# Batch 0's Q and K in thirds, w1 and w2 in quarters, and a first phase in another order

## The chip, the cores and the metric

The kernel runs on one core of a Trainium2 chip. The metric is the time of one execution in microseconds, measured on the device. A core has five engines that work through their own queues in order: TensorE (PE; its weight loads are PEld), VectorE (DVE), ScalarE (ACT), GpSimd (POOL) and SyncE (SP). They wait for each other by semaphores only. Transfers between HBM and SBUF run beside them on 16 DMA engines; an engine's queue only issues them.

## The reference

Attention over a sliding window of 64 tokens, then a feed-forward block that multiplies two projections:

```python
scores = (1 / np.sqrt(64)) * np.matmul(q, k.transpose(0, 1, 3, 2))   # q, k, v: 8 batches, 8 heads, 576 tokens, 64
rel = pos[:, None] - pos[None, :]
scores = np.where((rel >= 0) & (rel < 64), scores, -1e9)
attn = softmax(scores)
x = np.matmul(attn, v)              # laid out as 4608 tokens x 512
h = ((x @ w1) * (x @ w2)) @ w3      # w1, w2: 512 x 1024, w3: 1024 x 1024
out = h @ w_out                     # w_out: 1024 x 512, out: 4608 x 512, fp32
```

All inputs are fp32 in HBM. The kernel computes in fp16 with fp32 accumulation. Since nothing stands between `w3` and `w_out`, it folds them once into one matrix `wc = w3 @ w_out` (1024 x 512).

## The kernel before

The work has three kinds. **Attention** goes by batch; a batch has three segments of 192 query tokens (`SEGS`), and a segment two halves of four heads, numbered d = 0 to 47. For segment n, `scores(n)` multiplies K and Q into two PSUM tiles; `weigh(d)` takes Exp of one half on ACT and zeroes what lies outside the window, on POOL by two selects (`select`) or on DVE by one multiply with a band of ones and zeros (`bands`, made by `make_bands`); `values(d)` multiplies with V and, through Ln, Exp(-x) and a multiply on DVE, writes normalized columns of `xT`. V's tiles `v16s` hold ones beside V (`ones_of`), so that the row sums come out of the same matmuls. `copy_v` builds V blocks that overlap others. `keep_sums` writes the logarithms of the sums to a small tile on SP's queue, for a check at the end.

**Folding** (once): `fold_t(fc)` transposes a row block of w3 on PE (8 matmuls with the identity) and copies it out of PSUM; `fold_mm(fc, c0, c1, cp)` multiplies it with w_out into columns of `wc_sb`, and `cp` says which engine takes the result out of PSUM.

**Feed-forward** goes by group g of 512 tokens, nine in all: `ffn_ab(g, fc)` computes one block of 128 columns of both projections (64 matmuls of 512 columns for a whole group), copies one to SBUF on ACT and multiplies on DVE; `ffn_o(g, t)` multiplies 128 tokens with `wc_sb`, and `store` writes them out on SP's queue. `ffn_ab` and `fold_*` share four PSUM buffers (`ps_f`), `scores` and `values` share two (`ps_a`).

**Q and K** come in head pairs: `load_qk` loads a batch by four transfers per tensor (32 partitions each), converting to fp16 on the way, which POOL's queue does; `transposes(b, which, hh)` turns 32x32 blocks on DVE, one call per tensor and half hh (576 tokens), into `kT` and `qT`.

**Order.** Nothing is scheduled automatically (`manual_schedule`): each engine gets its instructions in the order of the Python calls. Every load that converts is issued by POOL. The loads share eight semaphores in turn, so a load waits at POOL for the landing of the load eight before it. The first phase, lines 516 to 619, is written out call by call: loads, `keep_busy(120)` (matmuls of the identity with itself, whose result nobody reads), scores of batch 0, folding, values, the first group's `ffn_ab`, and batch 1's attention between the first group's `ffn_o`. From line 622 on a loop takes over: `slots` lists what is left of the feed-forward with a due tick each, and `tick(u)` runs attention four ticks per segment between them, its loads by the table `late`.

Of the kernel before, what the change touches and what calls it, by code (L numbers as in the profile page):

```python
# [8 lines left out]
FP32 = mybir.dt.float32  # L9
# [135 lines left out]
def kernel(  # L145
# [25 lines left out]
    EARLY = 2  # L171
# [28 lines left out]
    RUN = [9] * 3 + [2] * (B - 3)  # L200

    def load_qk(b, which, *hhs):
        src = k if which == "k" else q
        r = RUN[b]
        if (which, b) not in t16s:
            t16s[which, b] = sb.tile([P, 2, TI * D], FP16, name=which + "16", bufs=2)
        t = t16s[which, b]
        if not hhs:
            for j in range(NJ):
                nc.gpsimd.dma_start(  # L210
                    out=t[32 * j:32 * j + 32].rearrange("p hh (i n) -> p (hh i) n", n=r * D),
                    in_=src[b, 2 * j:2 * j + 2].rearrange("hh (i p r) d -> p (hh i) (r d)", p=32, r=r))
        for hh in hhs:
            for i in range(2):
                nc.gpsimd.dma_start(
                    out=t[:, hh, i * r * D:(i + 1) * r * D],
                    in_=src[b, hh:H:2, i * 32 * r:(i + 1) * 32 * r].rearrange("j (p r) d -> j p (r d)", p=32, r=r))

    def transposes(b, which, hh):

        dst = kTs if which == "k" else qTs
        r = RUN[b]
        if hh == 0:
            dst[b] = sb.tile([P, 2, S, 2], FP16, name=which + "T")
        nc.vector.transpose(  # L225
            dst[b][:, hh].rearrange("q t c -> q (t c)").bitcast(I32).rearrange("q (i p r) -> q i r p", p=32, r=r),
            t16s[which, b][:, hh].bitcast(I32).rearrange("p (i r e) -> p i r e", r=r, e=32))
# [44 lines left out]
    def scores(n, now=True):  # L272
# [19 lines left out]
        weigh(2 * n)  # L292
        if now:
            weigh(2 * n + 1)

    def weigh(d):
# [9 lines left out]
        if d % 2 == 1 and d < 6 * EARLY:  # L306
# [7 lines left out]
    def values(d):  # L314
# [7 lines left out]
        o_ps = ps_a.tile([P, 2, 512], FP32, name="a_ps")  # L322
        if jp == 0:
            lns[b, si] = sb.tile([P, NJ, 192], FP32, name="ln_s", bufs=4)
        y = lns[b, si][:, j0:j0 + 2]
        r = sb.tile([P, 2, 192], FP32, name="r")
        x0 = (b * S + q_base) % RING
        xs = xT[:, j0:j0 + 2, x0:x0 + 192]
        if b < SHORT:
# [12 lines left out]
            o, total = (o_ps[:, e, 0:384].rearrange("p (j n) -> p j n", j=2) for e in range(2))  # L342
            nc.scalar.activation(y, total, AF.Ln)
            nc.scalar.activation(r, y, AF.Exp, scale=-1.0)  # L344
            nc.vector.tensor_tensor(xs, o, r, ALU.mult)  # L345
            return
        for jj in range(2):
            first = True
            for a in range(2):
                c0 = 0  # L350
                for bi, (k0, q0, n, _) in enumerate(seg):
# [6 lines left out]
                    c0 += n  # L358
        nc.scalar.activation(y[0:D], o_ps[D:P, :, 0:192], AF.Ln)  # L359
# [23 lines left out]
    def tick(u):  # L383
# [3 lines left out]
        if m == 0 and n < NS:  # L387
            scores(n, now=False)
        if m == 1 and n < NS:
            weigh(2 * n + 1)  # L390
        if m in (1, 2) and 6 < n <= NS:
            values(2 * n - 3 + m)
        for e in late.get(r, []):
            event(b, *e)
# [59 lines left out]
    def load_w12(i, half):  # L454
        cols = slice(half * 512, half * 512 + 512)
# [3 lines left out]
    def load_wo(half):  # L459
        cols = slice(half * 256, half * 256 + 256)  # L460
        nc.gpsimd.dma_start(out=wo16[:, :, cols], in_=moe_w_out[:, cols].rearrange("(e p) m -> p e m", p=P))  # L461

    def load_w3(n):
        fc = 2 * n
        dst = w3a[:, 2 * fc:2 * fc + 4, :].rearrange("p (f a) n -> p f (a n)", f=2) if n < 2 else \
            xT[:, fc - 4:fc - 2, 2 * S:2 * S + DF]
        nc.gpsimd.dma_start(out=dst, in_=moe_w3[fc * P:fc * P + 2 * P].rearrange("(f p) n -> p f n", p=P))

    def fold_t(fc):
# [6 lines left out]
        dve_cp(w3Ts[fc], tp)  # L476
# [49 lines left out]
    for i in range(2):  # L526
# [10 lines left out]
    load_w3(3)  # L537
    load_v(0, 4, 5)
    fold_mm(0, 0, 256, act_cp)
    fold_mm(1, 0, 256, act_cp)  # L540
    fold_t(2)
    fold_t(3)
    scores(2)
    for i in range(2):
        load_w12(i, 0)
    fold_mm(2, 0, 256, act_cp)
    fold_mm(3, 0, 256, act_cp)
    fold_mm(0, 256, DM, act_cp)
    fold_mm(1, 256, DM, act_cp)
    fold_t(4)  # L550
    fold_t(5)
    fold_mm(2, 256, DM, act_cp)
    fold_mm(3, 256, DM, act_cp)
    copy_v(0, 1)
    fold_mm(4, 0, DM, act_cp)
    values(0)
    values(1)
    fold_t(6)
    fold_mm(5, 0, DM, act_cp)
    values(2)  # L560
    values(3)
    copy_v(0, 4)
    fold_t(7)
    fold_mm(6, 0, DM, act_cp)
    values(4)
    values(5)
    fold_mm(7, 0, DM, act_cp)
    for i in range(2):
        load_w12(i, 1)
    load_qk(1, "k")  # L570
    load_qk(1, "q")
# [115 lines left out]
```

## Time and profile before

| what | us |
|---|---|
| median of 3 runs (268.27 to 270.63) | 268.4 |
| profiled execution | 268.59 |
| its span, first to last instruction | 266.8 |
| PE busy | 254.4 |
| DVE / ACT / POOL busy | 169.7 / 151.4 / 178.7 |

HBM is read for 38.8 MB and written for 9.44 MB. The granted clock of TensorE is 0.997 of full speed over the span.

How to read it: a row names the line of the kernel, the engine, the operation, and out<-in by the program's names with partitions x elements; x120 is the number of instructions. Times in the timeline and in the chain are microseconds from the start of the span. In square brackets stands how long the engine stood idle just before, and what ended the idle time. Matmuls are pipelined: a row's length is from the first start to the last end, and the next row can start before it ends. The line "GB/s" gives bytes as written (fp16 in SBUF) in 40 equal slices of the span, 6.67 us each. The tile names `ab` and `xT` of DMA rows in the first phase are w3 and w_out: their fp16 copies lie in buffers that are used otherwise later. L506 is `keep_busy`, L474 `fold_t`, L481 `fold_mm`, L286 `scores`, L337 the matmuls of `values`, L417 those of `ffn_ab`, L435 those of `ffn_o`, L225 the transposes on DVE, L210 the loads of Q and K.

### The profile page before, as it was taken

The page shows a single profiled execution, that of the slowest core. Times are in us where ns is not written, and L with a number is a line of the kernel's source. Part 1 is how long each engine was busy: PE and PEld are TensorE (multiplying, and loading weights), DVE is VectorE, ACT ScalarE, POOL GpSimd, SP SyncE. Part 2 cuts the span into 40 slices and gives each one's busy share as a digit, 9 for nine tenths or more (in the row PEclk, how much of TensorE's full clock was granted, in tenths as well). Part 3 has the DMA queues.
Part 4 walks back from the last instruction along what each step waited for, and adds up shares of the span by engine and source line. Part 5 has one row for each costly group of instructions (what it writes and reads, how often), then busy time and mean ns, then how long its engine had stood idle before and what let it go on. Part 6 is the DMA issues. An engine that isn't in the chain of part 4 may idle for free.

```text
span 266.8 us, 6600 instructions
## 1 busy us (share of the span) xinstructions
PE 254.4 (95%) x2608; PEld 149.7 (56%) x2608; DVE 169.7 (64%) x260; ACT 151.4 (57%) x261; POOL 178.7 (67%) x243
## 2 busy tenths in 40 slices
PE   3979999998999999999999999999999999999992
PEld 3968654445886445545556984545455445444441
DVE  6644454978775675986687567668786565564531
ACT  1037474367656577758874855777498748342300
POOL 7979826679879999999898739687766345005000
PEclk9999999999999999999999999999999999999998
DMA  5999999999999999899999765998540040012013
GB/s 81 170 207 186 189 207 201 131 181 138 149 106 62 131 206 77 61 165 162 62 106 180 102 43 64 202 105 57 99 96 4 7 150 6 0 53 108 0 57 109
DMA packets 75380, 29.45 MB, mean 110 GB/s; under 512 B 62369, under 2 KB 69793, under 8 KB 75345
## 3 DMA queue, kind: packets, MB, share of 16 engines
q0 software_dynamic: 69920, 19.41, 74.9%
q1 hardware_dynamic: 5280, 9.46, 10.0%
q8 instruction: 21, 0.34, 0.6%
q14 instruction: 15, 0.11, 0.2%
q10 hardware_dynamic: 144, 0.13, 0.1%
HBM read 38.80 MB, written 9.44 MB: 181 GB/s over the span
## 4 chain that ended last, share of the span: by engine, by line
PE 87%; DMA 4%; POOL 2%; DVE 2%; ACT 2%; issue 1%; POOLq 0%; DVEq 0%
PE f_ps L417 48%; PE f_ps L435 22%; PE a_ps L353 5%; PE a_ps L286 4%; PE f_ps L481 4%; DMA ab<-in_moe_w_dram 4%; PE a_ps L337 3%; ACT pt L303 1%; PE f_ps L474 1%; POOL q L210 1%; POOL k L210 1%; DVE xT L345 1%; DVE kT L225 1%; POOL ab L461 0%; DVE pt L308 0%
## 5 line engine op out<-in xcount | busy, mean ns | idle before, releaser
L417 PE MATMUL f_ps<-xT,w_sb 128*128 128x512 f16 (+1 forms) x704 | 131.5, 341 | 0.0
L417 PEld LDWEIGHTS <-w_sb 128*128 128x128 f16 x704 | 66.3, 98 | 50.7 <-issue 0.2
L423 DVE TENSOR_TENSOR ab<-f_ps,a_sb 128x512 f16<-128x512 f32 x72 | 49.6, 689 | 33.0 <-PE f_ps L417 31.2
L303 ACT ACTIVATE pt<-a_ps 128x1024 f16<-128x1024 f32 (+1 forms) x48 | 44.5, 953 | 45.4 <-PE a_ps L286 45.4
L258 POOL TENSOR_SCALAR_AFFINE_SELECT pt<-pt 128x1024 f16<-128x1024 f16 (+2 forms) x56 | 46.1, 824 | 30.6 <-ACT pt L303 30.5
L435 PE MATMUL f_ps<-wc_sb,ab 128*128 128x512 f16 (+1 forms) x296 | 66.4, 374 | 0.0
L422 ACT COPY a_sb<-f_ps 128x512 f32<-128x512 f32 x72 | 41.8, 581 | 36.9 <-PE f_ps L417 36.4
L260 POOL TENSOR_SCALAR_AFFINE_SELECT pt<-pt 128x1024 f16<-128x1024 f16 (+2 forms) x56 | 46.5, 831 | 3.9
L435 PEld LDWEIGHTS <-ab 128*128 128x128 f16 x296 | 27.3, 98 | 28.8
L238 POOL DMA_DIRECT2D v<-in_v_dram x40 | 34.0, 860 | 1.0 <-issue 0.4
L362 DVE TENSOR_TENSOR xT<-a_ps,r 64x384 f16<-64x384 f32 x30 | 16.5, 550 | 22.0 <-ACT r L361 22.0
L437 DVE COPY t2k<-f_ps 128x512 f32<-128x512 f32 (+1 forms) x35 | 23.7, 679 | 8.4 <-PE f_ps L435 7.9
L210 POOL DMA_DIRECT2D q<-in_q_dram x32 | 19.7, 621 | 11.8 <-DMA w_sb<-in_moe_w_dram 8.3
L210 POOL DMA_DIRECT2D k<-in_k_dram x32 | 20.1, 634 | 1.6 <-POOLq L671 1.0
L353 PEld LDWEIGHTS <-v 128*128 128x128 f16 x240 | 15.1, 98 | 6.4
L345 DVE TENSOR_TENSOR xT<-a_ps,r 128x384 f16<-128x384 f32 x18 | 10.0, 553 | 13.0 <-ACT r L344 13.0
L359 ACT ACTIVATE ln_s<-a_ps 64x384 f32<-64x384 f32 x30 | 14.6, 487 | 5.8 <-PE a_ps L353 5.0
L353 PE MATMUL a_ps<-pt,v 128*128 128x128 f16 x240 | 17.2, 215 | 0.0
L363 DVE TENSOR_TENSOR xT<-a_ps,r 64x384 f16<-64x384 f32 x30 | 16.8, 561 | 0.4
L286 PEld LDWEIGHTS <-kT 32*128 32x128 f16 x768 | 10.9, 92 | 9.6 <-issue 9.3
L361 ACT ACTIVATE r<-ln_s 128x384 f32<-128x384 f32 x30 | 15.7, 523 | 1.0
L225 DVE STREAM_TRANSPOSE qT<-q 128x576 int32<-128x576 int32 x16 | 14.7, 928 | 1.6 <-DMA q<-in_q_dram 1.6
(44 smaller groups left out, 184.9 us busy)
## 6 DMA issues: line engine op xcount, KB each, us to landing
out_dram<-t2k SPq DMA_DIRECT2D x35, 256.0 KB
k<-in_k_dram POOLq DMA_DIRECT2D x32, 144.0 KB, 6.3
q<-in_q_dram POOLq DMA_DIRECT2D x32, 144.0 KB, 5.8
v<-in_v_dram POOLq DMA_DIRECT2D x32, 128.0 KB, 5.0
w_sb<-in_moe_w_dram POOLq DMA_DIRECT2D x4, 512.0 KB, 9.7
ab<-in_moe_w_out_dram POOLq DMA_DIRECT2D x2, 512.0 KB, 9.5
ab<-in_moe_w_dram POOLq DMA_DIRECT2D x2, 512.0 KB, 9.4
xT<-in_moe_w_dram POOLq DMA_DIRECT2D x2, 512.0 KB, 10.4
```

Source lines behind the costliest of these rows:

```text
L210: nc.gpsimd.dma_start(out=t[32 * j:32 * j + 32].rearrange("p hh (i n) -> p (hh i) n", n=r * D), in_=src[b, 2 * j:2 * j + 2].rearrange("hh ...
L238: nc.gpsimd.dma_start(out=vh[lo:P, c], in_=v[b, :, s0:s0 + P - lo, :].rearrange("h s d -> s h d"))
L258: nc.gpsimd.affine_select(out=sl, in_=sl, pattern=pat, compare_op=ALU.is_ge, fill=0.0, base=off, channel_multiplier=-1)
L260: nc.gpsimd.affine_select(out=sl, in_=sl, pattern=[[-s, m] for s, m in pat], compare_op=ALU.is_ge, fill=0.0, base=63 - off, channel_multip ...
L286: nc.tensor.matmul(s_ps[j // 2][:, j % 2, o0:o0 + m], kT[part, a, k0:k0 + P, c], qT[part, a, q0:q0 + m, c], start=(c == 0), stop=(c == 1), ...
L303: nc.scalar.activation(pt[:, :, :, 0:w], s_ps, AF.Exp, bias=-SHIFT, scale=scale)
L353: nc.tensor.matmul(o_ps[:, jj, o0:o0 + n], v16[:, si * 2 + bi, j0 + jj, a * D:a * D + P], pt[:, jj, a, c0:c0 + n], start=first, stop=(bi = ...
L417: nc.tensor.matmul(d[:, f * n + c0:f * n + c1], w[:, dc, (fc + f) * P:(fc + f + 1) * P], xT[:, dc, xc:xc + c1 - c0], start=first, stop=(dc ...
L422: act_cp(a_sb[:, 0:nf * n], a_ps[:, 0:nf * n])
L423: nc.vector.tensor_tensor(ab[:, fc:fc + nf, lo:hi], b_ps[:, 0:nf * n].rearrange("p (f n) -> p f n", f=nf), a_sb[:, 0:nf * n].rearrange("p ...
L435: nc.tensor.matmul(o_ps[:, 0:c1 - c0], ab[:, fc, t * P:t * P + P], wc_sb[:, fc, c0:c1], start=(fc == 0), stop=(fc == 7))
L437: cp(o_sb[:, c0:c1], o_ps[:, 0:c1 - c0])
```

## The change

Batch 0's Q and K are cut into three thirds of 192 tokens (`RUN[0]` is 6 instead of 9). The first third of each tensor and half is loaded as fp32 without conversion, three of the four by SP's queue and one by ACT's, into a part of w1's tile (`room_of`); `cast` converts it on DVE or ACT. The other thirds come converted, by POOL (`load_third`). `transposes` can do one third. w1 and w2 are loaded in quarters of 256 columns instead of halves, w3 in five pieces instead of four. `values` is split: `norm` is a call of its own, made right behind it in the loop, so that nothing changes there. `weigh` gets its engine as an argument; batch 0 and 1 now have eight of twelve halves on DVE instead of six. `fold_t` gets the engine of its copy. One of the two memsets of ones goes to POOL. The first phase is laid out anew; the loop from tick 24 on is the same.

```diff
-    RUN = [9] * 3 + [2] * (B - 3)
+    RUN = [6] + [9] * 2 + [2] * (B - 3)
...
+    def third(b, which, hh, i):
+        r = RUN[b]
+        src = k if which == "k" else q
+        return src[b, hh:H:2, i * 32 * r:(i + 1) * 32 * r].rearrange("j (p r) d -> j p (r d)", p=32, r=r)
+
+    def room_of(which, hh, i):
+        n = RUN[0] * D
+        y = 2 * "kq".index(which) + hh
+        return (w1_sb, w2_sb)[i].rearrange("p a n -> p (a n)").bitcast(FP32)[:, y * n:(y + 1) * n]
...
+    def load_raw(which, hh, i, queue):
+        queue.dma_start(out=room_of(which, hh, i), in_=third(0, which, hh, i))
+
+    def cast(which, hh, i, cp):
+        n = RUN[0] * D
+        cp(t16_of(0, which)[:, hh, i * n:(i + 1) * n], room_of(which, hh, i))
+
+    def load_third(b, which, hh, i):
+        n = RUN[b] * D
+        nc.gpsimd.dma_start(out=t16_of(b, which)[:, hh, i * n:(i + 1) * n], in_=third(b, which, hh, i))
...
-        if d % 2 == 1 and d < 6 * EARLY:
+        if engine is nc.vector:
...
-    def load_w12(i, half):
-        cols = slice(half * 512, half * 512 + 512)
+    def load_w12(i, c0, c1):
+        cols = slice(c0, c1)
...
-    load_qk(0, "k")
+    load_w3(0, 1)
     make_identity(nc, ident16)
-    load_qk(0, "q")
-    load_wo(0)
-    load_w3(0)
+    load_w3(1, 1)
+    load_raw('k', 1, 0, nc.sync)
     make_bands()
-    load_w3(1)
-    load_wo(1)
-    load_w3(2)
-    load_v(0, 0, 2, 3)
-    for i in range(2):
-        ones_of(i, nc.vector)
-    for which in "kq":
-        for hh in range(2):
-            transposes(0, which, hh)
-    keep_busy(120)
-    scores(0)
-    keep_busy(30)
-    fold_t(0)
-    fold_t(1)
+    load_w3(2, 2)
+    load_raw('q', 1, 0, nc.sync)
+    load_wo(0, 256)
+    ones_of(1, nc.gpsimd)
+    load_third(0, 'q', 1, 1)
+    load_raw('k', 0, 0, nc.sync)
+    keep_busy(85)
+    cast('k', 1, 0, dve_cp)
+    load_wo(256, 512)
+    load_third(0, 'k', 0, 1)
+    load_raw('q', 0, 0, nc.scalar)
+    cast('q', 0, 0, dve_cp)
+    transposes(0, 'q', 0, 0)
+    load_w3(4, 2)
...
+    fold_t(0, act_cp)
+    fold_t(2, act_cp)
...
+    fold_t(1, dve_cp)
...
+    keep_busy(20)
+    fold_t(3, act_cp)
+    keep_busy(20)
+    fold_mm(2, 0, 256, act_cp)
+    load_third(0, 'q', 0, 2)
     scores(0)
+    weigh(0, nc.vector)
+    fold_mm(0, 0, 256, dve_cp)
+    transposes(0, 'k', 0, 1)
+    fold_mm(1, 0, 256, dve_cp)
...
+    load_w12(1, 512, 768)
+    values(3)
+    load_qk(1, 'k')
+    norm(3)
+    load_qk(1, 'q')
+    fold_mm(7, 0, DM, act_cp)
+    load_w12(0, 768, 1024)
+    fold_mm(6, 0, DM, act_cp)
+    load_w12(1, 768, 1024)
     scores(2)
+    load_qk(2, 'k')
+    weigh(4, nc.vector)
+    weigh(5, nc.vector)
+    ffn_ab(0, 0, 2, 0, 256)
+    values(4)
+    load_v(1, 0)
+    norm(4)
+    ffn_ab(0, 2, 2, 0, 256)
+    keep_sums(0)
+    values(5)
+    norm(5)
+    transposes(1, 'k', 0)
+    ffn_ab(0, 4, 2, 0, 256)
+    load_v(1, 2)
+    transposes(1, 'q', 0)
+    ffn_ab(0, 2, 2, 256, 512)
+    ffn_ab(0, 0, 2, 256, 512)
+    transposes(1, 'k', 1)
+    transposes(1, 'q', 1)
...
+    ffn_ab(0, 4, 2, 256, 512)
+    ffn_ab(0, 6)
+    ffn_ab(0, 7)
+    scores(3)
```

On PE the new order of the first phase is: 85 fillers; fold_t 0, 2, 1; 20 fillers; fold_t 3; 20 fillers; fold_mm 2 (first half); scores 0; fold_mm 0 and 1 (first halves), 1, 2, 0 (second halves); fold_t 4; fold_mm 3; fold_t 5; fold_mm 4; scores 1; fold_t 7; fold_mm 5 and 3; values 0, 1; fold_mm 5; fold_t 6; values 2, 3; fold_mm 7, 6; scores 2; then the first group's ffn_ab with values 4 and 5 between. On POOL the converting loads come in this order: w3 rows 0, 1, 2 and 3; w_out's first half; Q's second third of half 1; w_out's second half; K's second third; w3 rows 4 and 5; three thirds; w3 rows 6 and 7; V blocks 2, 0; a third; V block 3; a third; then quarters of w1 and w2 with the last third and V blocks 5 and 4 between; K and Q of batch 1; the last quarters of w1 and w2.

More of the change, by code (lines that the diff above doesn't have):

```diff
@@ L270, with scores @@
     held = {}
-    def scores(n, now=True):
+    def scores(n):
         b, si = divmod(n, 3)
@@ L605 @@
+    scores(5)
+    transposes(2, 'k', 1)
+    weigh(10, nc.vector)
+    ffn_o(0, 2, dve_cp)
+    weigh(11, nc.gpsimd)
+    values(6)
+    values(7)
+    store()
+    norm(6)
+    keep_sums(1)
+    norm(7)
+    keep_sums(2)
+    transposes(2, 'q', 1)
+    ffn_o(0, 3, act_cp)
+    copy_v(1, 4)
+    keep_sums(3)
+    load_v(2, 0)
+    values(8)
+    values(9)
+    norm(8)
+    norm(9)
+    transposes(2, 'q', 0)
+    store()
+    load_v(2, 5)
+    load_qk(3, 'k')
+    keep_sums(4)
     ffn_ab(1, 0, 2, 0, 256)
+    load_v(2, 2)
@@ L606 @@
+    load_qk(3, 'q')
     values(10)
-    transposes(2, "q", 1)
+    norm(10)
+    values(11)
+    norm(11)
+    keep_sums(5)
     ffn_ab(1, 2, 2, 0, 256)
-    values(11)
-    for n in range(3, 6):
-        keep_sums(n)
     U0 = 24
```

215 lines of the change are left out of this document (111 added, 104 removed).

## The prediction

> **What bounds the kernel now.** First the page, then the chain that ended last in order of time, then PE's rows in the timeline.
>
> The engine rows and the stream's rate (40 slices of 6.67 us):
> ```profile
> PE 254.4 (95%) x2608; PEld 149.7 (56%) x2608; DVE 169.7 (64%) x260; ACT 151.4 (57%) x261; POOL 178.7 (67%) x243
> ...
> GB/s 81 170 207 186 189 207 201 131 181 138 149 106 62 131 206 77 61 165 162 62 106 180 102 43 64 202 105 57 99 96 4 7 150 6 0 53 108 0 57 109
> ```
> PE is busy to the end, so time is saved only where PE stands still or does nothing useful. The rate is near its best from slice 2 to slice 7: summed, 1.67 MB are in at 13.3 us, 6.93 at 40, 8.27 at 46.7. That answers the program: K, Q, V of batch 0 (1.8 MB as fp16), the four weights (5.2), K and Q of batch 1 (1.2), together 8.2.
>
> The chain, cut to 0 to 68 us (start, length, what):
> ```profile
> 1.49 1.40 POOL k L210 x3
> ...
> 7.51 9.87 DMA ab<-in_moe_w_dram
> 17.38 0.05 issue
> 17.43 1.07 PE f_ps L474 x16
> ...
> 40.10 13.93 PE f_ps L417 x64
> ...
> 64.05 0.85 DVE kT L225
> ```
> Until 17.4 the chain is POOL's issues and the landing of the first w3 rows; afterwards PE with small pauses.
>
> PE's rows of the timeline (start, length, work, idle before):
> ```profile
> 4.57 9.02 PE L506 MATMUL f_ps<-ident 128*128 128x128 f16 x120 [4.57 <-POOL ident masks.py:199]
> ...
> 14.85 1.85 PE L506 MATMUL f_ps<-ident 128*128 128x128 f16 x30
> 17.43 1.07 PE L474 MATMUL f_ps<-ident,ab 128*128 128x128 f16 x16 [0.73 <-DMA ab<-in_moe_w_dram]
> ...
> 39.94 14.09 PE L417 MATMUL f_ps<-xT,w_sb 128*128 128x512 f16 x64
> ...
> 65.61 0.64 PE L337 MATMUL a_ps<-pt,v 128*64 128x128 f16 x16 [0.78 <-DVE xT L345]
> 66.18 1.92 PE L417 MATMUL f_ps<-xT,w_sb 128*128 128x256 f16 x16
> ```
> L506 is filler. From 17.43 to 39.94 PE has 21.7 us of real work (eight fold_t at 0.5, folds 14, two scores at 0.57, six values at 0.45), so it pauses only 0.8. What can be won is the time before 17.43, and some 2 us between 53.96 and 66.18.
>
> **The change, part by part.** All times count from the span's start.
>
> *Head of POOL.* Four K loads (0.81 and three of about 0.55) stand ahead of the identity; afterwards one w3 row (0.72, as L467). The filler starts at 3.0 instead of 4.57. 120 fillers take 9.02; 35 fewer at the 56 ns of the second block ((1.85 - 0.22) / 29) leave 7.1: PE is free at 10.1.
>
> *The stream.* The bytes to the last quarter of w2 are the same 8.2 MB. A third as fp32 (0.2 MB written) reads what a converted one reads; I count it as 0.1. First bytes come some 1.8 us after an issue (1.49; 0.54 MB by 6.67 at about 0.165 MB/us), a landing 1.4 after the last bytes (w3's first pair is byte 2.23 MB, in at 16.0 by the slices, used at 17.43). For w3, wo, w1, w2 I take the 0.205 of slices 3 and 6, for V 0.15. POOL issues w3 rows 2 and 3 at 6.5 (3.0, plus 0.7, plus make_bands, 2.75 today): in at 10.6, landed **12.0**. The same sum gives wo's first half 14.6, second 17.8, w3 rows 4 and 5 20.8, 6 and 7 24.8, w1's first quarter 34.9, Q of batch 1 **43.7**, w2's last 46.3.
> The memset of 128x3072 that goes to POOL has no row there: between 2.5 (POOL's 0.23 for 128 columns and 0.32 for 256, carried on by slope) and 3.9 (twelve of 0.32). I take 2.7, near DVE's 2.62 for the same shape. It hides behind wo's bytes in flight; at 3.9 the landings behind it are 1 later.
>
> *Casts and transposes.* Four casts of 384 columns have no row: at most DVE's 0.68 for 512 columns out of PSUM, at least 0.29 for its copy of 512 fp16 on 64 partitions; 0.45 taken. With four transposes of a third (1.21 / 3 = 0.4) and ones_of (2.6), DVE is done by about 11, before the first fold wants it. w1's loads now wait for the casts on POOL's queue, and everything POOL issues stands behind them; they are reached at about 20, so nothing waits.
>
> *PE's walk*, in the new order, with the rows' durations. fold_t(0) at 10.1, then 1.4 of standing still until fold_t(2) at 12.0; fold_t(1), 20 fillers (1.1), fold_t(3), 20 fillers: fold_mm(2) starts at 15.7, wo is there. By then four fold_t are done (2.0) and scores(0) is not (0.57): today PE is that far at 17.43 + 1.43 = 18.9. **3.2 won.** From here to the end of ffn_ab(0, 7): 34.4 of walk, made of the folds 14, four fold_t 2.0, three scores 1.7, six values 2.7 and 64 matmuls' worth of ffn_ab 14. Added: six ffn_ab in two halves of 256 columns take 1.85 (66.18 row) instead of 1.73, **0.7 lost**; values(4) stands right behind one ffn_ab after scores(2) and must wait for Exp (0.97) and the band multiply (0.75), **0.6 lost**; the pause of 0.8 today goes, as each landing above is ahead of its use by 0.1 to 1.1. DVE's transposes of Q of batch 1 now stand ahead of the multiplies of ffn_ab(0, 2) and (0, 0): PE goes on at landing plus 2.0 (1.21 and 0.69), 45.7 against its own 46.0, so no wait, but the two hh=1 transposes behind them hold the last buffer for **0.3**. ffn_ab(0, 7) ends at about 51.5 against 53.9: 2.4 won.
>
> *Second stage.* The same ffn_o, scores and values in the same order. The transpose at 64.05, which holds norm(7) and thus values(9), moves ahead of them; PE's pauses there (1.1 around 64.2, plus small ones) mostly go: **1.2 won**. POOL has two selects fewer (2.2 each) and one load of w3 and four of w1, w2 more (0.75 each), and follows. After tick 24 the order is today's, and all of it only starts earlier.
>
> Sum: 3.2 - 0.7 - 0.6 + 0.8 - 0.3 + 1.2 = 3.6. The profiled execution took 268.6 (span 266.8 and 1.8 around it), the median of the runs is 268.4: **265.0**.
>
> **Rivals.**
> *B, the stream is the bound.* PE would be ready, the bytes not. For it: all landings above have less than 1.1 to spare, and over slices 3 to 7, V's loads included, the rate is 0.198, not 0.205. Against: today's 1.67 MB in 13.3 us contain a slow head. If the stream only keeps today's pace, byte 7.67 (the last of Q of batch 1) is in at 43.7 (6.93 at 40, then 201 GB/s) and landed at 45.1; with 1 more for the POOL memset, 46.1. ffn_ab(0, 7) ends 7.6 behind that landing (2.0, then 1.73 + 3.9 through the held buffer): 52.7 to 53.7, 0.2 to 1.2 won, plus 1.2: 266.2 to 267.2, middle 266.8.
> [...]
>
> *C, more is won.* Rows 2 and 3 of w3 land with the filler's end (their bytes need 1.44 / 0.205 = 7 from 3.0, if make_bands is no brake), 1.4 more, and the 0.6 goes behind other work: 263.0.
>
> *D, slower: too few bytes in flight.* POOL has eight loads outstanding: at 34.67 to 42.77 each Q issue waits for the landing of a w_sb load eight before. The new order cuts the loads between w3's last rows and Q of batch 1 to 0.1 to 0.26 MB each. Eight small ones could starve the engines. Today's V loads with following K and Q show 131 GB/s in the slice from 46.7, with POOL waiting for V's landings. From 23.4, when w3's last rows are in (24.8 less 1.4), the stream carries 3.64 MB to byte 7.67; break-even with today is Q landing at 47.5, or 0.160 MB/us; at 0.14 it lands at 50.8, DVE's queue stands still behind the transpose and PE with it: 3.3 slower, 271.9. Against it: K and Q of batch 1, loads of 0.147 MB, ran at 201 GB/s in slice 7.
>
> *E, it does not do what it says:* the fp32 thirds land no earlier than today's K (8.3). Even at 12 scores(0) at 16.6 finds them cast and transposed; nothing changes in the sum.
>
> **How the numbers follow.** Forecast 50% (264 to 266.2), B 24% (266.2 to 269, the upper part where several of its delays add up), C 14% (261.5 to 264), D 12% (from 269). One per cent is 2.7 us, about what a measurement of this kernel can tell from no change: faster than 265.7 are C and some three quarters of the forecast's cases, 51%; within 1% the rest of it and B, 38%; slower over 1%, 11%. Range 262.2 to 269, which leaves out D and a little of C.
>
> **What would show it.** PE: filler from 3.0, fold_t(2) at about 12 with an idle of 1.4 ended by a DMA, fold_mm(2) at 15.7, ffn_ab(0, 0) at 35, scores(3) at 51.6, the second group's first ffn_ab at about 62.5 (66.18 today). Under B, PE's idle in 16 to 50 is ended by DMA or by DVE behind the Q transposes; under D the slices from 23 to 47 us show under 160 GB/s. The forecast is wrong if fold_t(2) waits far past 12, or if a wait of DVE's queue for a third holds back a fold's eviction.

## The result and the profile after

The changed kernel takes 278.6 us (median, 277.75 to 279.89), the kernel before 268.5 on the same chip: a ratio of 1.036, 95% interval 1.030 to 1.043. Forecast were 265.0 and a range of 262.2 to 269.0. The direction was wrong. The one slower rival, D, was priced at 271.9; its row "from 269" is open upwards and so holds the number, but what cost the 10.1 is not what D named (below).

The profiled execution took 278.74, its span 277.0. Its page, with the engines' busy time, TensorE's granted clock and the bytes written in 40 slices, here of 6.92 us:

```profile
PE 256.8 (93%) x2639; PEld 157.1 (57%) x2639; DVE 170.3 (61%) x270; ACT 156.1 (56%) x265; POOL 181.2 (65%) x243
...
PEclk9975999999999999999999999999999999999998
...
GB/s 107 167 203 159 127 115 113 184 179 158 133 165 124 58 140 215 59 80 180 126 36 146 196 66 2 142 156 59 97 143 4 1 79 76 1 40 114 0 43 120
```

PE does 2.4 more work than before and the span is 10.2 longer: PE stands still, or runs slowly (two slices at 0.7 and 0.5 of its clock). From slice 5 to 7 the stream carries 113 to 127 GB/s, where it carried 189 to 207 before.

PE's rows in the timeline of the changed kernel (start, length, work, in brackets the idle time before and what ended it). L532 is the filler, L500 `fold_t`, L507 `fold_mm`, L304 `scores`, L444 `ffn_ab`:

```profile
2.84 7.37 PE L532 MATMUL f_ps<-ident 128*128 128x128 f16 x85 [2.84 <-POOL ident masks.py:199]
10.05 0.61 PE L500 MATMUL f_ps<-ident,ab 128*128 128x128 f16 x8
15.02 1.89 PE L500 MATMUL f_ps<-ident,ab 128*128 128x128 f16 x16 [4.36 <-DMA ab<-in_moe_w_dram]
16.70 2.03 PE L532 MATMUL f_ps<-ident 128*128 128x128 f16 x20
21.28 0.69 PE L500 MATMUL f_ps<-ident,ab 128*128 128x128 f16 x8 [2.55 <-ACT w3T L502]
25.00 2.29 PE L532 MATMUL f_ps<-ident 128*128 128x128 f16 x20 [3.04 <-DVE w3T L502]
27.09 1.73 PE L507 MATMUL f_ps<-ab,w3T 128*128 128x256 f16 x8
...
64.47 0.53 PE L304 MATMUL a_ps<-qT,kT 32*128 32x128 f16 x32
...
76.51 1.92 PE L444 MATMUL f_ps<-xT,w_sb 128*128 128x256 f16 x16
```

The filler and fold_t(0) are where the forecast had them (3.0 and 10.1). Then fold_t(2) comes at 15.0 (forecast 12.0), two waits for copies follow, and fold_mm(2) comes at 27.1 (forecast 15.7). scores(3) is 10.5 later than before (64.47 against 53.96), the second group's first `ffn_ab` 10.3 (76.51 against 66.18), the end of the span 10.2: all of the loss arises ahead of scores(3). Some 8.2 of it are there when fold_mm(2) starts at 27.1, since the kernel before is that far with its work at 18.9 by the prediction's count.

The chain that ended last, in order of time (start, length, what), shows what the copies wait behind:

```profile
2.49 16.89 DMA w_sb<-in_k_dram
...
19.39 0.51 ACT k L230
19.90 0.42 ACT q L230
...
20.35 0.52 DVE qT L243
20.87 0.34 DVE kT L243
...
21.78 2.62 DVE v L538
24.40 0.56 DVE w3T L502
...
25.00 2.29 PE f_ps L532 x20
```

SP issues its last plain third at 2.49, and the cast on ACT that waits for it starts at 19.39, 16.9 later. ACT's copies of fold_t(0) and fold_t(2) stand behind the casts. DVE's transposes wait for the casts, the memset of ones (2.62) stands behind the transposes, and DVE's copy of fold_t(1) behind that.

### The profile page after: what moved, and what is told of

Same layout as the page of the kernel before. It is cut to its first block, busy times and chain, and to the rows that moved or that the text cites. A ratio compares the mean times of both kernels' runs of the same rounds, so it can differ in the third digit from the quotient of the medians.

```text
span 277.0 us, 6672 instructions
## 1 busy us (share of the span) xinstructions
PE 256.8 (93%) x2639; PEld 157.1 (57%) x2639; DVE 170.3 (61%) x270; ACT 156.1 (56%) x265; POOL 181.2 (65%) x243
## 3 DMA queue, kind: packets, MB, share of 16 engines
q1 hardware_dynamic: 5676, 10.05, 10.4%
## 4 chain that ended last, share of the span: by engine, by line
PE 71%; DMA 16%; DVE 5%; POOL 3%; issue 2%; ACT 1%; SPq 1%; DVEq 0%
PE f_ps L444 37%; PE f_ps L462 20%; DMA w_sb<-in_k_dram 6%; DMA w_sb<-in_moe_w_dram 5%; PE a_ps L358 4%; PE a_ps L304 3%; PE f_ps L507 3%; DMA v<-in_v_dram 3%; DMA q<-in_q_dram 2%; PE a_ps L346 1%; POOL k L206 1%; DVE v L538 1%; DVE kT L243 1%; DVE pt L323 1%; PE f_ps L532 1%
## 5 line engine op out<-in xcount | busy, mean ns | idle before, releaser
L444 PE MATMUL f_ps<-xT,w_sb 128*128 128x512 f16 (+1 forms) x752 | 131.7, 329 | 0.3 <-DVE ab L450 0.3
L444 PEld LDWEIGHTS <-w_sb 128*128 128x128 f16 x752 | 70.9, 98 | 46.2 <-issue 0.3
L450 DVE TENSOR_TENSOR ab<-f_ps,a_sb 128x512 f16<-128x512 f32 x72 | 49.4, 687 | 28.5 <-PE f_ps L444 26.0
L276 POOL TENSOR_SCALAR_AFFINE_SELECT pt<-pt 128x1024 f16<-128x1024 f16 (+2 forms) x53 | 43.6, 822 | 34.6 <-ACT pt L318 34.6
L318 ACT ACTIVATE pt<-a_ps 128x1024 f16<-128x1024 f32 (+1 forms) x48 | 44.5, 953 | 28.5 <-PE a_ps L304 28.4
L278 POOL TENSOR_SCALAR_AFFINE_SELECT pt<-pt 128x1024 f16<-128x1024 f16 (+2 forms) x53 | 43.9, 829 | 3.7
L464 DVE COPY t2k<-f_ps 128x512 f32<-128x512 f32 (+1 forms) x34 | 23.0, 680 | 8.3 <-PE f_ps L462 7.7
L206 POOL DMA_DIRECT2D q<-in_q_dram x28 | 17.7, 642 | 4.6 <-issue 3.9
L243 DVE STREAM_TRANSPOSE qT<-q 128x576 int32<-128x576 int32 (+1 forms) x20 | 15.5, 775 | 8.3 <-ACT q L230 8.2
L206 POOL DMA_DIRECT2D k<-in_k_dram x28 | 17.7, 654 | 0.0
L532 PE MATMUL f_ps<-ident 128*128 128x128 f16 x125 | 11.7, 281 | 5.9 <-DVE w3T L502 3.0
L386 ACT ACTIVATE r<-ln_s 128x384 f32<-128x384 f32 x30 | 15.7, 523 | 1.0
L304 PEld LDWEIGHTS <-kT 32*128 32x128 f16 x768 | 10.8, 92 | 9.5 <-issue 9.5
```

The lines of the kernel that those rows point to most:

```text
L206: nc.gpsimd.dma_start(out=t[32 * j:32 * j + 32].rearrange("p hh (i n) -> p (hh i) n", n=r * D), in_=src[b, 2 * j:2 * j + 2].rearrange("hh ...
L276: nc.gpsimd.affine_select(out=sl, in_=sl, pattern=pat, compare_op=ALU.is_ge, fill=0.0, base=off, channel_multiplier=-1)
L278: nc.gpsimd.affine_select(out=sl, in_=sl, pattern=[[-s, m] for s, m in pat], compare_op=ALU.is_ge, fill=0.0, base=63 - off, channel_multip ...
L304: nc.tensor.matmul(s_ps[j // 2][:, j % 2, o0:o0 + m], kT[part, a, k0:k0 + P, c], qT[part, a, q0:q0 + m, c], start=(c == 0), stop=(c == 1), ...
L318: nc.scalar.activation(pt[:, :, :, 0:w], s_ps, AF.Exp, bias=-SHIFT, scale=scale)
L444: nc.tensor.matmul(d[:, f * n + c0:f * n + c1], w[:, dc, (fc + f) * P:(fc + f + 1) * P], xT[:, dc, xc:xc + c1 - c0], start=first, stop=(dc ...
```

## The experiments

Theories at the start: **H**, the plain thirds land late and the casts that wait for them hold the folds' copies on ACT and DVE; **L**, the rest of the layout (small pieces, order) costs it; **C**, it is the lowered clock. Runs 1 to 4 sort these, 5 to 12 look for what H left over, 13 to 17 test the cause that came out. Runs 2, 3 and 4 are one execution each, beside 268.4 for the kernel before; the others are medians with the ratio's 95% interval.

**1. All thirds through POOL, no casts** (`e1_pool_thirds`, from the changed kernel; all four `load_raw` and casts go):

```diff
-    load_raw('k', 1, 0, nc.sync)
+    load_third(0, 'k', 1, 0)
+    load_third(0, 'q', 0, 0)
+    load_third(0, 'q', 1, 0)
+    load_third(0, 'k', 0, 0)
+    load_w3(2, 2)
+    load_wo(0, 256)
     make_bands()
-    load_w3(2, 2)
...
-    load_wo(0, 256)
...
```

> Takes the plain fp32 loads and the casts out: the four first thirds come converted by POOL, issued right behind the second w3 row; make_bands goes behind wo's first half; all else as changed. Theory H (the plain loads land late, and the casts that wait for them hold the fold's copies on ACT and DVE): fold_mm(2) starts at 15 to 17 us instead of 27.1, the time is 264 to 268. Theory L (the layout itself, quarters and small pieces): the folds may start early, but PE then waits for DMAs between 20 and 50, and the time stays over 274. [...]

Measured: 271.95, ratio 1.011 (1.009 to 1.014). The time lies in none of the ranges: 6.6 of the 10.1 go with the plain loads and casts, and 3.5 stay, more than H allowed. fold_t(2) still waits for w3, and fold_mm(2) comes at 19.35:

```profile
14.42 1.89 PE L500 MATMUL f_ps<-ident,ab 128*128 128x128 f16 x16 [4.23 <-DMA ab<-in_moe_w_dram]
```

**2. The casts behind the copies** (`e2_late_casts`; the plain loads stay where they are):

```diff
-    cast('k', 0, 0, act_cp)
...
-    cast('q', 1, 0, act_cp)
...
-    transposes(0, 'q', 1, 0)
...
-    transposes(0, 'k', 0, 0)
...
+    cast('k', 0, 0, act_cp)
+    cast('q', 1, 0, act_cp)
+    transposes(0, 'q', 1, 0)
+    transposes(0, 'k', 0, 0)
     scores(0)
```

> Keeps the plain loads, but ACT's two casts, and DVE's two transposes that follow them, stand behind fold_t's copies, right ahead of scores(0). H: the landing stays at 19 to 20, the folds no longer wait for it: fold_t(3) has no wait for ACT, fold_mm(2) starts at 20 to 22, the time is 272 to 274. L: 277 to 279, as PE only waits later for loads. If the landing moves with the casts, H is wrong in its first half.

Measured: 275.12. PE's rows:

```profile
21.92 1.03 PE L507 MATMUL f_ps<-ab,w3T 128*128 128x256 f16 x8 [0.70 <-DMA ab<-in_moe_w_out_dram]
25.13 0.53 PE L304 MATMUL a_ps<-qT,kT 32*128 32x128 f16 x32 [2.18 <-DVE kT L243]
```

fold_mm(2) comes 5.2 earlier, without a wait for a copy; scores(0) now waits for the same late thirds. The queueing is real and costs some 3.5 in this one execution, a little less than H's range (272 to 274) has it; the lateness itself remains.

**3. POOL's loads later** (`e3_raw_first`; identity, bands and ones ahead of POOL's first load, which goes from 1.4 to 6.7):

> POOL makes identity, bands and ones before its first load, so the plain loads of SP and ACT have the DMA engines alone until about 8 us. If they land late because POOL's converting loads crowd them out: DVE's first cast by 5 us, ACT's cast of K by 8. If a plain load of this shape is slow by itself: ACT's cast stays later than 14. The time says little, since all of POOL's loads start 6 us later: 274 to 282.

Measured: 274.73, although POOL's stream starts 5.3 later. The first cast starts at 8.11 and ACT's at 13.96:

```profile
13.96 0.51 ACT L230 CAST k<-w_sb 128x384 f16<-128x384 f32 x1 [11.77 <-DMA w_sb<-in_k_dram]
```

That is far from the 5 and 8 of loads that are only crowded out, and at the edge of what a slow shape would give. With POOL's stream beside them from the start, as in the changed kernel, the same loads take until 19.39, so the stream adds to the lateness. But at the 76 GB/s of the window below the 0.79 MB of the four loads take an estimated 10.3 us by themselves. The share of DMA in this kernel's window from 3 to 5 us, when only plain loads run, points at why (second last column: 1.00 is 16 engines busy, and a little more where packets overlap; the last is GB/s):

```profile
3.00:5.00 2.00, 2.00 (x21) 2.00 (x20) 0.00 (x0) 0.00 (x0) 1.86 (x4) 1.00 0.23 76
```

**4. The clock kept up** (`e4_warm`; 75 more fillers between fold_t(0) and fold_t(2)):

> As changed, with 75 fillers more between fold_t(0) and fold_t(2), in the 4.4 us in which PE stands still; nothing else moves. C: the granted clock stays near 1.00 between 15 and 30 and the time falls by 3 or more, to 275 or less. H: PE then waits longer for the same copies; only the fillers and the fold behind the last wait (25.0) get faster, 1.8 us: 276.5 to 277.5.

Measured: 276.49, as H had it. fold_t(2) and (1) now run at the full clock (1.07 for the pair instead of 1.89; 1.07 also in the kernel before, at a granted 1.00), and PE waits all the longer for the copy behind ACT's casts:

```profile
21.51 2.29 PE L536 MATMUL f_ps<-ident 128*128 128x128 f16 x20 [5.85 <-ACT w3T L502]
```

Behind this wait 20 fillers, fold_t(3) and 20 more fillers take 2.29, 1.06 and 2.29, where run 13 has 1.28, 0.61 and 1.28 for them. So the run moves the lowered clock and does not remove it; what the clock is worth it does not tell. It does tell that C is not the cause: with PE on time, the copies hold it up as before.

**5. Halves for thirds** (`e5_halves`; the first run's kernel with `RUN[0]` 9, 8 loads with rows of 1152 bytes instead of 12 with 768):

> As e1_pool_thirds, but Q and K of batch 0 in two halves of 288 tokens (rows of 1152 bytes, as in the kernel before) instead of three thirds (768 bytes, with 390 packets of 4 bytes each in the trace): first halves where the first thirds stood, second where the second stood. Theory T (the thirds' packets slow the stream): although 0.2 MB more must be in before w3 rows 2 and 3, these land no later than the 14.4 of e1, Q of batch 1 lands earlier than there, and the time falls to 269 to 271. If the thirds are no dearer than their bytes: w3 rows 2 and 3 land at 15.5 and the time is 272 to 273.

Measured: 273.03, ratio 1.014 (1.010 to 1.017); fold_t(2) at 15.15. Not the rows' length.

**6. The quarters alone** (`e6_quarters`; the kernel before, each half of w1 and w2 in two loads):

> The kernel before with one part of the change alone: w1 and w2 in quarters of 256 columns (eight loads instead of four), nothing else. If small loads behind eight semaphores starve the engines (rival D of the prediction): w2's last columns land 2 or more later than 42.8 and the time rises to 270 to 272. If not: 268 to 269.

Measured: 268.25, ratio 0.999 (0.997 to 1.002). The quarters cost nothing.

**7. The folds first, no thirds** (`e7_folds_first`; w3 and w_out's first half ahead of K and Q, these in halves through POOL):

> The idea of the new order without plain loads and thirds: w3's rows and w_out's first half first, Q and K of batch 0 by POOL in halves, folding from about 10 us on, weigh of batch 0 on DVE, w1 and w2 in quarters, and the second stage in the order of before with the transpose of K moved behind norm(7). If what cost the ten was the plain loads, the thirds and what waits for them: fold_t from 9.5 us, the first group's ffn_ab ends at 50 to 53 (53.9 before), the time is 264.5 to 267.5. If any early folding is held back by loads: 268 or more.

Measured: 271.67, ratio 1.011 (1.006 to 1.016). It has neither plain loads nor casts nor a lowered clock in its first phase (20 fillers take 1.28 there and 32 matmuls of the folds 3.67, as in run 13 and in the kernel before), and loses nearly as much as run 1 (3.0 and 3.5). Common to runs 1, 5 and 7 is the form of batch 0's loads.

**8. That form alone** (`e8_form`; the kernel before, which has the code for it but does not use it):

```diff
-    load_qk(0, "k")
+    load_qk(0, "k", 0, 1)
...
-    load_qk(0, "q")
+    load_qk(0, "q", 0, 1)
```

A load then takes one head half and half of the tokens, `"j (p r) d -> j p (r d)"`: four groups of 32 rows into 128 partitions, instead of one head pair with four rows in each of 32 partitions. Bytes, row length, number and order of loads stay.

> The kernel before with one thing changed: batch 0's K and Q come in four loads per tensor by head half and token half (128 partitions, rows of 1152 bytes) instead of four by head pair (32 partitions); bytes, number of loads and order stay. It measures by itself the form in which the thirds and halves were loaded. If the form is slow (the rate of 99 to 126 GB/s seen while thirds were being written, instead of about 165), 1.2 MB take up to 4 us longer: the first fold_t moves from 17.4 to 20 or 21 and the time is 270.5 to 272. If a load costs what its bytes cost whatever its form, fold_t starts at 17.2 to 17.7 and the time is 268 to 269; then the rest of what the kernel with thirds through POOL lost has to come from its order.

Measured: 272.33, ratio 1.015 (1.013 to 1.017): 3.8 for eight loads in another form. The first fold_t comes at 20.50 instead of 17.43:

```profile
17.22 3.38 PE L506 MATMUL f_ps<-ident 128*128 128x128 f16 x30
20.50 1.09 PE L474 MATMUL f_ps<-ident,ab 128*128 128x128 f16 x16
```

Not all of these 3.1 are a slower transfer. POOL's eight issues take 5.63 instead of 4.59, so up to 1.0 is issue time. The filler ahead of fold_t starts 2.4 later and takes 3.38 instead of 1.85 (113 ns a matmul instead of 62, from which I estimate a clock of about half) behind two pauses of PE for Q's transposes (0.91 and 1.25); 0.7 of the 3.1 comes from that, the rest of this cost being hidden in the wait of 0.73 that the kernel before has there. The window from 3 to 5 us, first of the kernel before, then of this one (columns as above):

```profile
3.00:5.00 2.00, 0.43 (x5) 0.44 (x6) 1.41 (x2) 0.00 (x0) 1.92 (x5) 1.00 1.07 143
```

```profile
3.00:5.00 2.00, 0.00 (x0) 0.00 (x0) 1.41 (x2) 0.00 (x0) 1.92 (x6) 1.00 0.50 31
```

And the packets on the two pages, in the same order:

```profile
DMA packets 75380, 29.45 MB, mean 110 GB/s; under 512 B 62369, under 2 KB 69793, under 8 KB 75345
```

```profile
DMA packets 78451, 29.46 MB, mean 109 GB/s; under 512 B 65440, under 2 KB 72864, under 8 KB 78416
```

The same bytes with 3071 more packets, in the trace 4 bytes long: 384 to a load. The share of 0.23 in run 3 is 3.7 of 16 engines, so I estimate that a load in this form uses four. Of its 128 rows each would then have 32, and 384 is 12 times 32, a packet of 4 bytes for each row that the other 12 do not have; the trace gives no packet an engine, so this is not shown. The trace does tell how many rows are in flight at once: of ACT's plain third in the changed kernel 2.7 on average, of batch 0's K and Q in the kernel before some 15. The four plain thirds of the changed kernel together, on two queues, never have more than 6 rows in flight. This is theory **F**: in the form of the thirds a load runs on four of the 16 engines.

The share of 0.50 does not say four by itself, for the packets of 4 bytes are counted in it; it goes with 31 GB/s, the 1.07 of the kernel before with 143. And POOL's thirds in this form, of which several are outstanding, reach 20 rows in flight in the changed kernel: by this estimate they do not all stand on the same four engines, as the plain ones seem to.

**9. The second stage's transpose** (`e9_transpose_behind`; the kernel before, `transposes(2, "k", 1)` moved behind `values(7)`):

> The kernel before with one call moved: the second transpose of K of batch 2 stands behind values(7) with its norm instead of ahead of it. This is the cause that the prediction gave for its last term (1.2 won in the second stage). If that holds, norm(7) comes about 1.1 earlier, the pause of 0.78 of PE ahead of values(9) goes and the time is 267.2 to 267.9. If something else is late next there (ACT's chain of Ln and Exp, POOL's selects of the segment), the pause is only renamed and the time is 268.2 to 268.6.

Measured: 267.76, ratio 0.998 (0.996 to 1.000). Again (`e9_again`):

> The kernel before with the one transpose moved, again and on the same chip as the run beside it: 267.4 to 268.2 if its ratio of 0.998 is real, the kernel before's own time otherwise.

267.24, ratio 0.997 (0.995 to 0.999). The stretch from scores(3) to the second group's `ffn_ab` takes 11.25 and 11.27 instead of 12.22, and PE's pause of 0.78 ahead of values(9) is gone (`e9_again`):

```profile
64.31 1.08 PE L337 MATMUL a_ps<-pt,v 128*64 128x128 f16 x32
65.33 1.92 PE L417 MATMUL f_ps<-xT,w_sb 128*128 128x256 f16 x16
```

Small, but in both intervals: the fastest kernel of the study, and less than one per cent.

**10. The whole second stage of the changed kernel behind the first of the kernel before** (`e10_second_stage`):

> The kernel before up to the end of the first group's ffn_ab, then the changed kernel's layout from scores(3) to tick 24 (V of batch 1 already loaded in the first phase). It tells the second stage's share by itself. By the prediction's last term 1.2 is won: 267.0 to 267.6. By the trace of the changed kernel, in which this stretch took 12.04 against 12.22 and a pair of band multiplies 3.4 beside POOL's selects, it is 268.0 to 268.7; a loss of over 1 would mean that the first phase hid something of the second's.

Measured: 268.34, ratio 1.000 (0.997 to 1.002). The stretch takes 11.18, 1.0 less. It is given back at 79.6, where DVE, with the multiply that PE waits for behind it, waits for V of batch 2, whose loads this grafted order issues later:

```profile
78.25 0.29 DVE L262 COPY v<-v 64x512 f16<-64x512 f16 x1 [5.74 <-DMA v<-in_v_dram]
```

**11. The folds first, with K and Q by head pair** (`e11_folds_by_pairs`):

> The order with the folds first again, but batch 0's K and Q whole and by head pair (32 partitions, as the kernel before loads them) behind w_out's first half, w1 and w2 in halves, the copies of w3T ahead of the norms on DVE, and from values(0) on the sequence of the kernel before. If the form of the loads and the order on DVE are what cost that kernel 3.2, it gives 267 to 269: the first 2.7 MB are the same bytes, and no order of them brings the last one earlier. If starting with the folds costs by itself, it stays at 270.5 to 272.5. Below 267 would mean that the order does win something once the form is mended.

Measured: 273.04, ratio 1.015 (1.012 to 1.018): worse than run 7 and above both ranges. With small loads behind large ones POOL stands at its limit of eight loads outstanding. POOL's row of the third wait, and PE's for what was issued behind it (w_out's second half, at 19.04):

```profile
15.78 0.54 POOL L206 DMA_DIRECT2D q<-in_q_dram  x1 [3.68 <-DMA ab<-in_moe_w_out_dram]
```

```profile
25.66 2.92 PE L507 MATMUL f_ps<-ab,w3T 128*128 128x256 f16 x16 [2.45 <-DMA ab<-in_moe_w_out_dram]
```

**12. Run 1 with its thirds by head pair**, 24 loads instead of 12 (`e12_thirds_by_pairs`):

> The changed kernel with all thirds through POOL, as measured before at 271.95, but every third loaded by head pair (32 partitions, both halves in one load, four loads per tensor and third: 24 loads of 98 KB read instead of 12 of 196 KB). If the form of the loads is what was left of the loss, w3 rows 2 and 3 land at 12.5 to 13.5 instead of 14.4 and the time is 268 to 270.5, although POOL issues twelve loads more (0.55 each). If it is the size of the loads or POOL's issues, it is 272 or more.

Measured: 285.49, ratio 1.059 (1.056 to 1.063). It says nothing about the form: scores(0) waited 8.98 for a transpose of a first third that DVE began only at 29.06, when a later third of K had landed. Run 15 gives each third a tile of its own, and that wait is gone.

**13. The changed kernel, only its plain thirds in the other form** (`e13_plain_by_pairs`):

```diff
+    def load_raw(which, queue):
...
+        for j in range(NJ):
+            queue.dma_start(out=room[32 * j:32 * j + 32].rearrange("p (hh n) -> p hh n", hh=2),
+                            in_=src[0, 2 * j:2 * j + 2, 0:32 * RUN[0]].rearrange("hh (p r) d -> p hh (r d)", p=32))
...
+    load_raw('k', nc.sync)
+    load_raw('q', nc.scalar)
```

> The changed kernel with the same plain thirds, each tensor in four loads by head pair (32 partitions, both halves) instead of two by head half (128 partitions), K on SP's queue, Q on ACT's; all else stays. Theory F: a load whose rows come as 4 groups of 32 in 128 partitions runs on four of the 16 engines only (the share of DMA is 0.23 of 16 engines where only plain loads run, and 0.50 against 1.07 for the converting loads in that form). Then in the other form the plain thirds are in by 6 to 8, ACT's first cast stands before 9 instead of 19.4, no fold copy waits for a cast, and the time is 270 to 273 (the thirds through POOL keep the slow form). Rival G: plain loads are late because POOL's stream leaves them a small part of the engines, whatever their form. Then ACT's cast stays behind 14 and the time above 274.5.

Measured: 269.88, ratio 1.007 (1.003 to 1.010), so 8.7 of the 10.1 come back. ACT's first cast and PE's rows:

```profile
8.63 0.51 ACT L236 CAST k<-w_sb 128x384 f16<-128x384 f32 x1 [6.45 <-DMA w_sb<-in_k_dram]
```

```profile
12.33 1.07 PE L506 MATMUL f_ps<-ident,ab 128*128 128x128 f16 x16 [1.99 <-DMA ab<-in_moe_w_dram]
...
16.18 1.28 PE L538 MATMUL f_ps<-ident 128*128 128x128 f16 x20 [1.22 <-DVE w3T L508]
17.30 1.04 PE L513 MATMUL f_ps<-ab,w3T 128*128 128x256 f16 x8
```

The cast stands at 8.6 instead of 19.4 while POOL's stream runs beside it. G, that POOL's stream crowds the plain loads out whatever their form, falls. The edit also spreads the loads evenly over two queues and makes eight of four; but with two queues in the old form too the rows in flight never passed 6. The window from 2.5 to 4 us has a DMA share of 1.06 and 230 GB/s here, 0.45 and 98 in the changed kernel. w3's rows 2 and 3 are in at 12.3, where the forecast had 12.0.

**14 and 15. The converting thirds by head pair too** (`e14_all_by_pairs`, from run 13; `e15_pool_by_pairs`, run 1's kernel):

> The same, and POOL's thirds by head pair too (16 loads of 98 KB read instead of 8 of 196 KB; each third in a tile of its own, so that no wait is taken for another third's bytes). F: the stream runs on 16 engines throughout and the time falls further, to 268 to 271; below 267.5 would mean that the layout is worth what it was forecast to be once its loads have another form. Rival: eight small loads outstanding hold too few bytes, POOL stands still at each of them, and it is 272 or more.

> The kernel with all thirds through POOL (271.95), by head pair, each third in its own tile: the run with 24 loads again without its wait of 17.7 on a later third. F alone: w3 rows 2 and 3 in at 12.5 to 13.5 instead of 14.4, 268.5 to 270.5. If the eight-load limit with loads of 49 KB written is what counts (POOL stood 1.55 there), they stay at 14.5 to 15.5 and it is 272 to 275.

Measured: 271.51 (ratio 1.010, 1.007 to 1.013) and 276.07 (1.026, 1.021 to 1.032). Run 14 lies between the range of F and that of its rival, run 15 above both; neither gains what F promised. What the rival named, POOL standing still at the limit of eight, is there. POOL's rows of run 14:

```profile
16.80 1.06 POOL L248 DMA_DIRECT2D k<-in_k_dram  x2 [2.32 <-DMA ab<-in_moe_w_out_dram]
...
20.89 1.06 POOL L248 DMA_DIRECT2D k<-in_k_dram  x2 [1.22 <-DMA ab<-in_moe_w_out_dram]
```

Four issues of together 2.25 also stand where one of 0.82 stood. So POOL issues w3's rows 4 and 5 at 17.85 instead of 12.71 in run 13, and PE waits 1.72 for them. In these two orders more and smaller loads on POOL's queue cost more than their form gave back; what the form alone gives there is not shown.

**16. Run 13 with both memsets of ones first on DVE** (`e16_ones_first`):

> The changed kernel with its plain thirds by head pair (269.88) and, beside that, both memsets of ones ahead of everything on DVE, where the kernel before has them (DVE has nothing to do there until 8.6), instead of one on POOL between two loads and one on DVE ahead of a fold's copy. What is left of the forecast's gain should come back: the wait of 1.22 for that copy goes (fold_mm(2) at 16.0 instead of 17.3) and POOL's loads from w_out's second half on are issued 2.7 earlier. If that is all that stood between the layout and its forecast: 266.5 to 268, so faster than the kernel before by up to 0.7 per cent. If the stream holds PE later anyway (waits ended by DMA between 20 and 40), 268.5 to 270.

Measured: 268.44, ratio 1.001 (0.998 to 1.003). PE's rows:

```profile
12.74 1.07 PE L506 MATMUL f_ps<-ident,ab 128*128 128x128 f16 x16 [2.50 <-DMA ab<-in_moe_w_dram]
...
17.95 1.04 PE L513 MATMUL f_ps<-ab,w3T 128*128 128x256 f16 x8
...
31.97 0.78 PE L352 MATMUL a_ps<-pt,v 128*64 128x64 f16 x28 [1.46 <-DVE v L268]
...
55.27 0.53 PE L310 MATMUL a_ps<-qT,kT 32*128 32x128 f16 x32
...
66.40 1.92 PE L450 MATMUL f_ps<-xT,w_sb 128*128 128x256 f16 x16
```

The time lies just below the second range, but PE has no wait that a DMA ends between 20 and 40. With its loads mended and the memsets moved, the layout is level with the kernel before: it loses 1.3 up to scores(3) (55.27 against 53.96) and wins 1.1 behind it (11.13 against 12.22). So little of the ten is left for L.

**17. Run 16 without the pause** (`e17_warm_ones_first`; 42 more fillers ahead of fold_t(2)):

> The kernel of the run before (268.44) with 42 more fillers, into the same PSUM buffer, where PE stood still for 2.5 ahead of fold_t(2), so that the clock does not fall (it was granted 0.66 from 13 to 18 there). fold_mm(2) then starts at 16.2 to 16.6 instead of 17.95. If that comes through to the end: 266.4 to 267.5, faster than the kernel before. If values(0) still waits for V's copy and the stream holds PE elsewhere, the gain is eaten by longer waits: 268 to 268.6.

Measured: 269.86, ratio 1.005 (1.002 to 1.008), above both ranges. fold_mm(2) starts at 17.11 and scores(3) at 54.16, 1.1 earlier than in run 16, but values(2) and values(8) then wait 1.14 and 1.32, and the second group starts at 66.58. The profiled execution, at 268.39, is the fastest of this kernel's eight; what the slower ones add the profile does not show.

## Why the prediction was wrong

*The stream*, first failed step. "I count it as 0.1" and the landings that follow took for granted that a third moves at the rate of its bytes. Neither the plain nor the converting thirds do, in their form (0.23 of 16 engines; 3.8 for eight converting loads, issue time and clock included). They hold back others too: w3's rows 2 and 3, whose own form never changed, land at 15.02 in the changed kernel and at 12.33 in run 13, with the same bytes issued ahead. 12.33 is close to the 12.0 of this step, so the counting of bytes was right, and the rate of the thirds was not. The trace of before held no load in this form, since `load_qk` uses it for no batch. What could be seen without a run were the patterns in the diff; the rate that goes with them only the runs showed.

*Casts and transposes* and rival *E*, second failed step. "DVE is done by about 11" and "nothing changes in the sum" looked at scores(0), which the thirds are for, and not at what stands behind the casts on ACT and DVE: the copies of fold_t(0), (2) and (1). The first thirds were late by E's own measure (casts at 10.4 to 19.4, not 8.3). Their standing ahead of the copies cost some 3.5 by itself (run 2), and with w3's late rows and what followed 8.7 (run 13), instead of nothing. The casts' own length was right (0.36 to 0.51 for 0.45). The prediction named the sign ("a wait of DVE's queue for a third holds back a fold's eviction") and gave it no price.

*PE's walk.* The one pause was forecast at 1.4 and was 4.36; the clock fell to 0.51 behind it (14.8 to 18.2) and to 0.50 behind the first of the two waits for copies (21.7 to 28.5). Behind the last of them 20 fillers and fold_mm(2) took 2.29 and 1.73 instead of 1.28 and 1.04 (run 13), 1.7 that no step had. In the mended kernel of run 16 the walk from fold_mm(2) to scores(3) takes 37.3, against 35.9 forecast. Waits of 1.46 for V's copy (within values(0)) and 0.49 (values(2)) are in it; the 0.6 for values(4) and the 0.3 for the held buffer, which the forecast had as losses, do not show as waits of PE. Its start, 17.95 instead of 15.7, makes the rest: 0.7 from the landing, 1.5 from the lowered clock (0.66 from 13 to 18). Together these are 3.7, the whole forecast gain of the first phase (2.4) and more.

*Second stage.* 1.2 forecast, 1.1 measured in runs 13 and 16 and 0.95 to 0.97 in run 9, by the mechanism named. In the changed kernel itself it was 0.2 (12.04): two band multiplies there took 3.41 together.

*Head of POOL* was right: the filler from 2.84, the memset on POOL 2.68 for 2.7.

*Rivals.* D, too few bytes in flight, was wrong where it was put: the quarters cost nothing (run 6). Its sign is nevertheless there, 159, 127, 115 and 113 GB/s in slices 4 to 7 of the changed kernel. But in the changed kernel POOL stood 4.60 for a late landing of w_out and 4.67 for a late Exp; with the same quarters and the same thirds on POOL, run 13 has 0.33 and no wait at these two places (15.85 and 31.59). Waits at the limit of eight are seen where loads are small (3.68 in run 11, 2.32 in run 14, 1.65 in run 15). B came nearest for the mended kernel, 268.4 against 266.8, by its number alone: in run 16 no DMA ends a wait of PE from 16 to 70 us.

The plain thirds on SP's and ACT's queues and POOL's stream did hold each other up: ACT's cast starts at 13.96 in run 3, where POOL's stream starts 5.3 later, and at 19.39 in the changed kernel beside it. This does not give the loss by itself, for in run 13 the same bytes on the same two queues, beside POOL's stream, left ACT's cast at 8.63 and cost 8.7 less.

What the sum looks like by runs: 278.6, less 8.72 for the form of the plain thirds with all that waited for them (run 13), less 1.44 for the memsets ahead of a copy and between loads (run 16), gives 268.44, the time before. What the form of POOL's thirds still costs in there is open: eight such loads alone cost 3.8 at the head of the kernel before (run 8), but the one way tried to mend them on POOL made more loads and lost (runs 12, 14, 15).

## What to carry to other kernels

Read a new load's access pattern as closely as its bytes. If its outermost dimension is 4, look in the profile at the share of DMA while it runs alone (0.23 here, run 3), before its landing is worked out from a rate. A cheap instruction that waits for a transfer can cost what stands behind it on its engine (3.5 here, run 2), so put it behind everything that does not need it, or make sure of the landing. More and smaller loads mended the form on SP's and ACT's queues (run 13); on POOL's, where a load waits for the one eight before it, they lost (runs 14 and 15).

## What was unexpected in the hardware

- The form of a load set its rate: a share of 0.23 of 16 engines and 76 GB/s with plain loads of 4 x 32 rows alone (run 3), 0.50 and 31 for converting ones (run 8), 1.07 and 143 for the same bytes as 32 partitions x 4 rows (the kernel before), each from 3 to 5 us. In the slow form each converting load of run 8 adds 384 packets of 4 bytes.
- A pause of PE of 4.36 was followed by 15 us, with two more pauses of 2.55 and 3.04 in them, at an average granted clock of 0.65 to 0.67. Narrower windows show it near 0.50 or near 1.00: 0.51 from 14.8 to 18.2, 0.99 to 21.7, 0.50 to 28.5. Behind a pause of 2.50 (run 16) the clock was 0.66 on average from 13 to 18, behind one of 1.99 (run 13) 1.00 in the same window. Behind one of 2.45 (run 11) fold_mm and scores took 2.92 and 1.04, where the kernel before has 1.92 and 0.64 for them; behind one of 2.18 (run 2) scores took 0.53, as in run 13. The windows of the changed kernel (PE busy first, the clock third from the right):

```profile
15.00:20.00 5.00, 3.71 (x36) 3.59 (x37) 0.00 (x0) 0.61 (x2) 0.67 (x1) 0.67 1.32 212
20.00:25.00 5.00, 0.69 (x8) 0.52 (x8) 4.03 (x4) 3.06 (x4) 1.66 (x2) 0.67 1.24 178
25.00:30.00 5.00, 5.00 (x68) 4.27 (x68) 0.00 (x0) 1.05 (x2) 3.81 (x5) 0.65 1.23 122
```

  The stretches at 0.50 in the changed kernel last 3.4 and 6.8. What sets their start and their length no run shows.
- DVE's band multiply of 128x1024 took 0.69 alone (run 16, at 40.99) and 2.18 beside POOL's issue of a V load and the selects behind it (run 13, at 31.08), a copy of V 1.87 instead of 0.29 beside the same (run 16, at 30.05), a cast 1.91 instead of 0.36 beside POOL's memset (run 13, at 8.65). It is not each time so: in the kernel before a multiply beside two selects took 0.69 (at 21.15). No run tests what decides it.
